# Segment-recurrent attention on one core: turns, scores and memory rows in 128x32 column tiles, the softmax's output turned by VectorE

## The chip, the cores and the metric

The kernel runs on one core of a Trainium2 chip. The metric is the device time of one execution in microseconds (us); where three runs are shown, it is their median. Engines are named as the profile names them: PE is TensorE (PEld its weight loads), DVE is VectorE, ACT is ScalarE, POOL is GpSimd, SP issues most DMAs.

A matmul on PE loads up to 128x128 stationary values (`lhsT`) and streams the columns of the moving operand (`rhs`) through them. The array can be used as smaller tiles: `tile_position=(row, column)` says which part a matmul uses. The profile writes a tile as rows * columns, so `128*32` is a matmul on all 128 rows and 32 of the 128 columns; four such tiles fit side by side.

## The reference

Two independent parts, whose outputs stand side by side. Part A is a sliding-window attention; the change does not touch it. Part B goes over 2048 tokens in 64 segments of 32, in strict order, and hands 8 memory rows from each segment to the next:

```python
for s in range(n_seg):
    xs = x[:, s * seg_len:(s + 1) * seg_len, :].copy()
    h = jnp.concatenate([mem, xs], axis=1)            # 8 + 32 tokens of width 640
    q = jnp.einsum('btd,dhe->bhte', h, Wq)            # 32 heads of 192
    k = jnp.einsum('btd,dhe->bhte', h, Wk)
    v = jnp.einsum('btd,dhe->bhte', h, Wv)
    scores = jnp.einsum('bhqe,bhke->bhqk', q, k) * scale
    scores = jnp.where(mask[None, None], scores, -1000000000.0)
    p = _softmax(scores, axis=-1)
    o = jnp.einsum('bhqk,bhke->bhqe', p, v)
    o = jnp.einsum('bhte,hed->btd', o, Wo)
    mem = o[:, :M, :].copy()
    outs.append(o[:, M:, :])
```

## The kernel before

`part_a` computes part A in about the first 150 us and loads weights for part B meanwhile. `part_b` calls `segment(s)` 64 times.

**Tokens and groups.** A segment has L = 40 tokens. Of the 32 that are projected in the segment itself (`main`), 8 are memory rows and 24 belong to x. The other 8, the last tokens of the segment, do not depend on the memory and are projected ahead for four segments at once (`ahead`, 32 tokens): once in four segments each group of Q, K and V is *renewed*, and the later segments take their 8 tokens from stored blocks (`Lb`, `Lv`); POOL copies such a block into QT or KT (L488). The 32 heads go in four groups of eight, g = 0 to 3.

**Projection** (`project32`, L443). The stationary operand is 32 tokens, the moving one 384 weight columns; four matmuls in four 128x32 column tiles make 32 tokens x 1536 columns. Five such rounds (the width 640 in chunks of 128) make 20 matmuls. The result has tokens on partitions, 32 for each of four pairs of heads. It is copied to bf16 (`to_sb`, L423).

**Turns** (`turn`, L456). Q and K are needed with head elements on partitions. Three 128x128 matmuls against an identity turn the 128x384 copy; `spread` copies the outcome into QT or KT, which hold, for each of the four pairs of heads, three chunks of 128 elements: head 0's first 128, the middle chunk with 64 elements of each head, and head 1's last 128.

**Scores** (`scores`, L515). 16 matmuls per group, eight on 128x64 tiles (the outer chunks) and eight on 64x64 tiles (the halves of the middle chunk), since each half of the middle chunk belongs to another head. The two heads of a pair lie on 64 partitions each.

**Softmax** (`softmax`, `put_p`, L522 to L540): on DVE scale and mask, maximum, subtraction; exponential on ACT; sum, reciprocal and two products on DVE, which write P. **Turn of P** (`turn_p`, L547): two 128x128 PE transposes into PSUM and a copy to PT (L423).

**Mix** (`mix`, L564): P times V, 16 matmuls on 32x128 tiles and 16 on 32x64 tiles into four PSUM tiles, copied to OT. **Output projection** (`project_out`, L578): 128x64 tiles, 320 columns, 24 matmuls per group (six pairs of chunks). **Memory rows** (`memory_rows`, L589): six matmuls turn the 8 new memory rows into HX, from which the next segment's projections start; `turn_late` for the next segment's Q follows.

**What sets the order.** PE runs in the order in which `segment` is written (`manual_schedule` for PE). On DVE, ACT, POOL and SP the framework's scheduler decides the order, and each engine then runs it strictly. Copies out of PSUM alternate between ACT and DVE by a counter (`evacuate`). PSUM buffers: 3 for projections (`ps_acc`), 4 that turns, scores, P's turn, mix and memory rows share in rotation (`ps_x`), 1 for the output (`ps_y`). QT, KT, P, PT, OT exist once. 23 weight tiles per segment (320 or 384 KB) do not fit in SBUF and are streamed from DRAM through five buffers (`get_unit`, L394), in PE's order.

## Time and profile before

| | |
|---|---|
| median of three runs | 2029.89 us (2027.99 to 2030.7) |
| the profiled execution: own time, span | 2024.66 us, 2022.8 us |
| PE busy | 1945.4 us, 96% of the span, 42512 matmuls |
| PE weight loads busy | 1243.6 us, 61% |
| DVE busy | 1128.3 us, 56% |
| ACT busy | 725.6 us, 36% |
| POOL busy | 193.6 us, 10% |
| DMA | 596.29 MB, mean 295 GB/s |
| mean granted TensorE clock | 0.994 |

How to read it: the page gives each engine's busy time, the chain of work that ended last followed back from the end, and groups of instructions by source line. A line of the timeline gives the start, the time from the first start to the last end of merged instructions, engine, source line, operation, output<-input, the tile, the size of the operand and the number of instructions; an idle time before it stands in brackets with what ended it. Matmuls are pipelined and their ends modelled, so the distance between starts says more about PE than its busy share. In a table by windows each engine has its busy time, then follow the granted clock, the busy share of the DMA engines and GB/s.

### The profile page before, as it was taken

The page shows a single profiled execution, that of the slowest core. Times are in us where ns is not written, and L with a number is a line of the kernel's source. Part 1 is how long each engine was busy: PE and PEld are TensorE (multiplying, and loading weights), DVE is VectorE, ACT ScalarE, POOL GpSimd, SP SyncE. Part 2 cuts the span into 40 slices and gives each one's busy share as a digit, 9 for nine tenths or more (in the row PEclk, how much of TensorE's full clock was granted, in tenths as well). Part 3 has the DMA queues.
Part 4 walks back from the last instruction along what each step waited for, and adds up shares of the span by engine and source line. Part 5 has one row for each costly group of instructions (what it writes and reads, how often), then busy time and mean ns, then how long its engine had stood idle before and what let it go on. Part 6 is the DMA issues. An engine that isn't in the chain of part 4 may idle for free.

```text
span 2022.8 us, 97144 instructions
## 1 busy us (share of the span) xinstructions
PE 1945.4 (96%) x42512; PEld 1243.6 (61%) x42512; DVE 1128.3 (56%) x3622; ACT 725.6 (36%) x2126; POOL 193.6 (10%) x674
## 2 busy tenths in 40 slices
PE   7989999999999999999999999999999999999998
PEld 4656666666666666666666666666666665666665
DVE  5875555555555455555555555555555554555554
ACT  3543333333333333333333333333333333333333
POOL 2000000110001101001001001101001001110110
PEclk9999999999999999999999999999999999999999
DMA  9927999999899999999999989999899988989997
GB/s 343 311 76 269 311 300 305 301 302 307 290 305 304 299 288 312 302 304 303 303 299 297 308 292 311 305 303 299 296 298 303 298 304 284 303 293 300 305 302 257
DMA packets 270123, 596.29 MB, mean 295 GB/s; under 512 B 61065, under 2 KB 72841, under 8 KB 269385
## 3 DMA queue, kind: packets, MB, share of 16 engines
q1 hardware_dynamic: 264770, 585.97, 87.9%
q8 instruction: 333, 5.46, 1.1%
q0 software_dynamic: 4928, 4.11, 0.6%
q14 instruction: 92, 0.75, 0.1%
HBM read 576.85 MB, written 18.87 MB: 295 GB/s over the span
## 4 chain that ended last, share of the span: by engine, by line
PE 71%; DMA 19%; DVE 6%; ACT 1%; issue 1%; SPq 1%; POOL 0%; DVEq 0%; POOLq 0%; ACTq 0%
PE acc L443 33%; PE Y L578 18%; DMA t<-wcopy_k 8%; DMA t<-wcopy_o 6%; PE pt L456 6%; PE Sps L515 4%; PE OTps L564 4%; PE pq L95 2%; PE pt L547 2%; DVE sb L423 2%; DMA out_dram<-row 2%; DMA t<-wcopy_v 1%; PE po L161 1%; DMA wcopy_o<-in_B_Wo_dram 1%; PE py L172 1%
## 5 line engine op out<-in xcount | busy, mean ns | idle before, releaser
L443 PEld LDWEIGHTS <-HX 128*32 128x32 bf16 x19380 | 462.7, 96 | 274.3 <-issue 46.5
L578 PEld LDWEIGHTS <-OT 128*64 128x64 bf16 x6144 | 316.8, 109 | 131.0 <-ACT OT L423 20.0
L578 PE MATMUL Y<-wres_o,OT 128*64 128x320 bf16 x3584 | 344.3, 302 | 2.2
L443 PE MATMUL acc<-wres_q,HX 128*32 128x384 bf16 x6460 | 332.6, 328 | 0.5 <-ACT sb L423 0.2
L443 PE MATMUL acc<-t,HX 128*32 128x384 bf16 x4200 | 309.1, 328 | 12.9 <-DMA t<-wcopy_k 10.1
L578 PE MATMUL Y<-t,OT 128*64 128x320 bf16 x2560 | 277.7, 303 | 10.0 <-DMA t<-wcopy_o 9.2
L423 DVE CAST sb<-acc 128x384 bf16<-128x384 f32 x322 | 178.8, 556 | 186.6 <-PE acc L443 171.3
L443 PE MATMUL acc<-wres_v,HX 128*32 128x384 bf16 x4844 | 276.5, 328 | 0.1
L528 ACT ACTIVATE t<-t 128x160 f32<-128x160 f32 x256 | 86.1, 336 | 439.4 <-DVE t L527 439.4
L443 PE MATMUL acc<-wres_k,HX 128*32 128x384 bf16 x3876 | 224.8, 327 | 0.3 <-issue 0.3
L522 DVE SCALAR_TENSOR_TENSOR t<-Sps,mask 128x160 f32<-128x160 f32 x256 | 82.8, 323 | 214.6 <-PE Sps L515 186.6
L423 ACT CAST sb<-acc 128x384 bf16<-128x384 f32 x324 | 153.6, 474 | 125.1 <-PE acc L443 123.5
L456 PE MATMUL pt<-ident,sb 128*128 128x128 bf16 x1938 | 179.4, 221 | 6.9 <-DVE sb L423 1.7
L423 DVE CAST OT<-OTps 128x120 bf16<-128x120 f32 x512 | 125.5, 271 | 97.4 <-PE OTps L564 96.8
L488 POOL COPY QT<-Lb 128x96 bf16<-128x96 bf16 x252 | 67.4, 267 | 1112.0 <-PE Sps L515 955.2
L456 PEld LDWEIGHTS <-sb 128*128 128x128 bf16 x1938 | 110.2, 97 | 82.3 <-issue 32.3
L515 PEld LDWEIGHTS <-QT 128*64 128x64 bf16 (+1 forms) x4096 | 118.9, 109 | 55.1 <-issue 40.5
L423 ACT CAST OT<-OTps 128x120 bf16<-128x120 f32 x512 | 106.0, 258 | 110.7 <-PE OTps L564 110.4
L515 PE MATMUL Sps<-KT,QT 128*64 128x40 bf16 (+1 forms) x4096 | 137.0, 188 | 2.2 <-DVE KT L423 1.0
L530 DVE TENSOR_REDUCE sm<-t 128x4 f32<-128x160 f32 x256 | 81.8, 320 | 78.7 <-ACT t L528 78.7
L564 PEld LDWEIGHTS <-Vst 32*128 32x128 bf16 (+1 forms) x4096 | 62.2, 97 | 82.3 <-issue 60.5
L564 PE MATMUL OTps<-PT,Vst 32*128 32x40 bf16 (+1 forms) x4096 | 109.7, 192 | 0.0
(75 smaller groups left out, 1916.0 us busy)
## 6 DMA issues: line engine op xcount, KB each, us to landing
t<-wcopy_o SPq DMA_DIRECT2D x640, 320.0 KB, 4.3
t<-wcopy_k SPq DMA_DIRECT2D x512, 384.0 KB, 4.8
t<-wcopy_v SPq DMA_DIRECT2D x320, 384.0 KB, 4.8
wres_q<-in_B_Wq_dram SPq DMA_DIRECT2D x20, 384.0 KB, 7.7
wres_v<-in_B_Wv_dram SPq DMA_DIRECT2D x15, 384.0 KB, 7.8
wres_k<-in_B_Wk_dram SPq DMA_DIRECT2D x12, 384.0 KB, 7.7
wres_o<-in_B_Wo_dram SPq DMA_DIRECT2D x14, 320.0 KB, 6.7
wcopy_o<-in_B_Wo_dram SPq DMA_DIRECT2D x10, 320.0 KB, 8.1
```

What stands on the lines that cost most here:

```text
L95: nc.tensor.matmul(pq[32 * d:32 * d + 32], lhsT=wcol[:, k, t, 4 * c + d, :], rhs=xTs[s][:, k, :], start=(k == 0), stop=(k == 4), tile_posi ...
L423: (nc.scalar.copy if copies["n"] % 2 else nc.vector.tensor_copy)(dst, src)
L443: nc.tensor.matmul(ps[n][32 * j:32 * j + 32, :], lhsT=X[:, dc, :], rhs=w[:, 384 * j:384 * j + 384], start=(dc == 0), stop=(dc == 4), tile_ ...
L456: nc.tensor.matmul(pt[:, c], lhsT=sb[:, 128 * c:128 * c + 128], rhs=ident, start=True, stop=True)
L488: nc.gpsimd.tensor_copy(tokens(T)[:, :, 32:L], b[:])
L515: nc.tensor.matmul(Sps[64 * g2:64 * g2 + 64, a, :], lhsT=QT[lo:hi, L * cc:L * cc + 64], rhs=KTt[lo:hi, cc, :], start=(g2 not in seen), sto ...
L522: nc.vector.scalar_tensor_tensor(out=t1[:], in0=Sps[:], scalar=scale, in1=mask[:].unsqueeze(1).to_broadcast([128, 4, L]), op0=ALU.mult, op ...
L528: nc.scalar.activation(t1[:], t1[:], ACTF.Exp)
L530: nc.vector.tensor_reduce(out=sm[:], in_=t1[:], axis=AX.X, op=ALU.add)
L547: nc.tensor.transpose(pt[:, late, :], P[:, late].rearrange("p a n -> p (a n)"), ident)
L564: nc.tensor.matmul(dst, lhsT=V[32 * a:32 * a + 32, e0:e1], rhs=PT[32 * a:32 * a + 32, late, half, :], start=(wide and late == 0 and half = ...
L578: nc.tensor.matmul(Y[64 * gv:64 * gv + 64, :], lhsT=OT[:, L * c:L * c + 64], rhs=w[:, n:n + 320], start=(i == 0 and r == 0), stop=(i == 23 ...
```

## The change

- `turn` makes each 128x128 turn in four matmuls on 128x32 column tiles (`turn32`), twelve per call in place of three. For K, the middle chunk's halves are directed to different places, so that the output's lower 64 partitions hold the chunks in one order and the upper 64 in another.
- KT is now [128, 4, 4, L]: the middle chunk of a pair of heads is kept twice, with zeros in the half that belongs to the other head (KT is cleared once at the start). `spread` therefore fills KT with two copies of 64 partitions each, where there was one of 128; POOL's copies of stored K blocks double in the same way.
- `scores` uses 128x32 column tiles alone: 32 matmuls per group, on full 128 rows. The 40 tokens of a head lie as two blocks of 32 rows (tokens 0 to 31; 32 to 39 and 24 unused rows) on the 32 partitions of a pair of heads. The mask is laid out to match.
- P has the same layout, so that a 32x32 block transpose on DVE (`nc.vector.transpose`, 128x256) makes PT in SBUF. `turn_p`, its PE transposes and its copies are gone; `put_p` returns PT.
- `memory_rows` uses 20 matmuls on 128x32 tiles in place of six on 128x128 and 128x64.
- In `segment`, `put_p` of groups 1, 2 and 3 stands behind the mix of the group before; the calls of `turn_p` are gone.

```diff
-    mask = cpool.tile([128, L], FP32)
+    mask = cpool.tile([128, 2, L], FP32)
...
-    KT = cpool.tile([128, 12 * L], BF16, name="KT")
+    KT = cpool.tile([128, 4, 4, L], BF16, name="KT")
-    P = cpool.tile([128, 2, 4, 32], BF16, name="P")
+    P = cpool.tile([128, 2, 2, 2, 32], BF16, name="P")
...
+    nc.gpsimd.memset(KT[:], 0.0)
...
-    def turn(sb):
+    def turn32(dsts, src):
+        for j in range(4):
+            nc.tensor.matmul(dsts[j][32 * j:32 * j + 32, :], lhsT=src[:, 32 * j:32 * j + 32], rhs=ident, start=True,
+                             stop=True, tile_position=(0, 32 * j))
+
+    LOW, HIGH = (1, 0, 2), (0, 2, 1)
+
+    def turn(sb, m):
         pt = ps_x.tile([128, 3, 4, 32], FP32, tag="x")
+        at = [pt[:, c].rearrange("p j n -> p (j n)") for c in range(3)]
         for c in range(3):
-            nc.tensor.matmul(pt[:, c], lhsT=sb[:, 128 * c:128 * c + 128], rhs=ident, start=True, stop=True)
+            lo, hi = (at[LOW[c]], at[HIGH[c]]) if m == "k" else (at[c], at[c])
+            turn32((lo, lo, hi, hi), sb[:, 128 * c:128 * c + 128])
         return pt
...
+    def heads(m, n0, n1):
+        if m == "q":
+            return [tokens(QT)[:, :, n0:n1].rearrange("p (j c) n -> p j c n", c=3)]
+        return [KT[0:64, :, 0:3, n0:n1], KT[64:128, :, 1:4, n0:n1]]
+
+    def spread(dsts, src):
+        for d, dst in enumerate(dsts):
+            part = src if len(dsts) == 1 else src[64 * d:64 * d + 64]
+            evacuate(dst.rearrange("p j c n -> p c j n"), part)
...
-        Sps = ps_x.tile([128, 4, L], FP32, tag="x")
...
+        Sps = ps_x.tile([128, 2, 2, L], FP32, tag="x")
+        plan = [(kind, g2, part) for kind in range(2) for g2 in range(2) for part in range(2)]
+        for n, (kind, g2, part) in enumerate(plan):
+            for a in range(4):
+                c = 3 * a + g2 + part
+                at = L * c + 32 * kind
+                nc.tensor.matmul(Sps[32 * a:32 * a + 32, g2, kind, :], lhsT=QT[:, at:at + 32],
+                                 rhs=KT[:, a, ((1, 0), (3, 2))[g2][part], :], start=(n == 0), stop=(n == len(plan) - 1),
+                                 tile_position=(0, 32 * a))
...
-    def turn_p():
-        pt = ps_x.tile([128, 2, 128], BF16, tag="x")
-        for late in range(2):
-            nc.tensor.transpose(pt[:, late, :], P[:, late].rearrange("p a n -> p (a n)"), ident)
-        PT = one.tile([128, 2, 2, L], BF16, tag="PT")
-        evacuate(PT[:], pt[:].rearrange("p l (h n) -> p l h n", h=2)[:, :, :, 0:L])
+        PT = one.tile([128, 2, 2, 64], BF16, tag="PT")
+        nc.vector.transpose(PT[:].rearrange("p l g n -> p (l g n)"), P[:].rearrange("p l g k n -> p (l g k n)"))
         return PT
...
-        for dc in range(5):
-            for gv in range(2):
...
+        for n in range(20):
+            gv, j = n // 10, n % 4
+            nc.tensor.matmul(pt[32 * j:32 * j + 32, n // 4, :], lhsT=Ysb[:, 32 * n - 320 * gv:32 * n - 320 * gv + 32],
+                             rhs=ident[:, 64 * gv:64 * gv + M], start=True, stop=True, tile_position=(0, 32 * j))
...
-        put_p(s, 0, *softmax(scores(0)))
+        PT[0] = put_p(s, 0, *softmax(scores()))
...
-        PT[0] = turn_p()
-        put_p(s, 1, *soft)
         tk[2] = project_qk(s, "k", 2)
         mix(0, PT[0], V[0])
+        PT[1] = put_p(s, 1, *soft)
         V[1] = values(s, 1)
         tk[2]()
-        PT[1] = turn_p()
```

Groups 2 and 3 change in the same way.

## Prediction

> **What bounds the kernel now.** I read the page first (busy shares, slices, chain), then the order of time on PE, DVE's order of time, last the DMA windows.
>
> ```profile
> span 2022.8 us, 97144 instructions
> PE 1945.4 (96%) x42512; PEld 1243.6 (61%) x42512; DVE 1128.3 (56%) x3622; ACT 725.6 (36%) x2126; POOL 193.6 (10%) x674
> PE 71%; DMA 19%; DVE 6%; ACT 1%; issue 1%; SPq 1%; POOL 0%; DVEq 0%; POOLq 0%; ACTq 0%
> ```
>
> PE carries the chain. Part B has 64 segments; the copy of the memory rows marks them:
>
> ```profile
> L592 DVE CAST HX<-pt x63: 199/200/202, 217.2 to 1990.5; 128x40 bf16<-128x40 f32 x63
> ```
>
> 62 steps in 1773.3 us are 28.60 us a segment. A busy PE is not a full PE, so I looked at starts (first column) in one segment:
>
> ```profile
> 1015.26 0.34 PE L456 MATMUL pt<-ident,sb 128*128 128x128 bf16 x3
> 1015.53 1.00 PE L443 MATMUL acc<-wres_q,HX 128*32 128x384 bf16 x20
> 1016.36 0.34 PE L443 MATMUL acc<-t,HX 128*32 128x384 bf16 x4
> ...
> 1020.08 0.50 PE L443 MATMUL acc<-t,HX 128*32 128x384 bf16 x8
> 1020.51 0.55 PE L515 MATMUL Sps<-KT,QT 128*64 128x40 bf16 x16
> 1020.99 0.68 PE L456 MATMUL pt<-ident,sb 128*128 128x128 bf16 x9
> ```
>
> Twenty projection matmuls start every 0.041 (0.83/20): four column tiles side by side. Turns add 0.057 each (0.34 for three, 0.68 for nine), so three should end 0.17 after their start; the next projection starts 0.27 after. Eight projections need 0.33, yet the scores follow after 0.43. Wherever the tile shape changes, about 0.10 passes with nothing running. A change inside one group:
>
> ```profile
> 1002.82 0.22 PE L564 MATMUL OTps<-PT,Vst 32*128 32x40 bf16 x8
> 1002.88 0.21 PE L564 MATMUL OTps<-PT,Lv 32*128 32x40 bf16 x8
> 1003.02 0.23 PE L564 MATMUL OTps<-PT,Vst 32*64 32x40 bf16 x8
> 1003.07 0.20 PE L564 MATMUL OTps<-PT,Lv 32*64 32x40 bf16 x8
> 1003.21 0.83 PE L443 MATMUL acc<-wres_v,HX 128*32 128x384 bf16 x16
> ```
>
> The step within one shape is 0.06, across the shapes 0.14. 32 matmuls with their 32 weight loads pass in 0.39, two such changes included. The turn of P inside an output projection:
>
> ```profile
> 1009.88 0.44 PE L578 MATMUL Y<-wres_o,OT 128*64 128x320 bf16 x4
> 1010.25 0.28 PE L547 MATMUL pt<-ident,P 128*128 128x128 bf16 x2
> 1010.47 0.33 PE L578 MATMUL Y<-wres_o,OT 128*64 128x320 bf16 x2
> ```
>
> 0.59 from output group to output group instead of 0.27.
>
> **The change, part by part (us per segment).**
>
> *Changes of shape.* In the program's order I count 39 per segment before. After it, turns, scores and memory rows have the projections' shape, and 20 are left (around the four mixes, three output projections and the two scores that border one). Of the 19 that go, three lie around the memory rows, where PE waits for the cast of Y anyway (30.2 in total, 0.47 a segment): I credit 0.1 there. The other 16 at 0.10: **-1.6**, and -0.1 at the end.
>
> *P on VectorE.* Eight matmuls of 0.057 leave PE: **-0.45**. Four copies of P leave (DVE 0.234 or ACT 0.292 each), four DVE transposes of 256 columns come. None is in the trace; DVE rows give 0.187 for 32 elements, 0.289 for 128, 0.320 for 160, 0.556 for 384, so 0.29 to 0.56, and by the line through them 0.42, which I take. The transpose also waits until the mix before has read PT; what stands behind it on DVE then is that mix's output or V, which come no earlier. PE's waits for P (two rows, 6.1 and 13.9, 0.3 a segment) mostly go: **-0.2**, the rest moves to the mix.
>
> *Scores.* 16 matmuls in two shapes become 32 in one. Without the two changes they take 0.25 now. Bounds for 32 in eight rounds of four: 0.009 each (the mix without its changes: 0.28) down to 0.005, the streaming of 40 columns at the projections' rate, and up to 0.023 (the row above, 0.36/16): 0.15 to 0.74. I take 0.19, near the low end, because four column tiles side by side is what the projections do: 4 x -0.06 = **-0.2**.
>
> *Turns and memory rows.* Three matmuls become twelve, in three rounds of 128 columns: 384 columns take a round 0.163, 128 a third, 0.055. Ten turns a segment: **0**. Memory rows, 20 for 6, go into the wait for Y: 0. Both with the same upper bound as the scores.
>
> Together **-2.4**. Now what is late next.
>
> *The copy of the second K projection.* In the row above it ends at 1020.58, a DVE cast of it runs 1020.70 to 1021.26, and its turn can start at 1021.31, 0.90 after PE streamed the last column (1020.41). PE fills that now with scores (0.48 with changes), a turn (0.17) and its first change, 0.75. After: 0.19 + 0.17. So 0.4 of the gain comes back as a wait: **+0.4**. The scores before it meet a K that is now copied in two halves (0.55 on DVE, 0.48 on ACT, side by side, but one behind the cast of Q): up to 0.3, inside the same wait.
>
> *The copy of the third Q projection.* In the built program DVE runs it behind the reciprocal of the first softmax:
>
> ```profile
> 1021.18 0.32 DVE L522 SCALAR_TENSOR_TENSOR t<-Sps,mask 128x160 f32<-128x160 f32 x1
> 1022.01 0.55 DVE L423 CAST KT<-pt 128x384 bf16<-128x384 f32 x1
> 1023.54 0.18 DVE L531 RECIPROCAL sm<-sm 128x4 f32<-128x4 f32 x1
> ```
>
> 2.36 from the first row to the reciprocal, with three casts between, 0.18, cast 0.48 in the stream, 0.05: 3.05 after the softmax begins. PE now gets there in wait, turn, two projections (1.63) and scores: 2.5 to 2.7. **+0.3**, in three of four segments.
>
> *Slots.* A mix holds four of four ps_x buffers; the next turn needs the first back, and its copy is behind the second softmax on DVE: **+0.2**. Half K copies ahead of the third and fourth scores: **+0.1**. POOL's copies into K double (189 more of 0.27), early in a stretch of over 2 us between scores: 0. If that cover were gone, 0.3.
>
> *DMA.* PE waits 21 in all for tiles. The columns end with DMA share and GB/s:
>
> ```profile
> 180.00:205.00 25.00, 23.41 (x552) 14.90 (x544) 12.78 (x44) 9.10 (x28) 0.00 (x0) 1.00 1.02 364
> 245.00:1990.00 1745.00, 1700.11 (x38553) 1088.97 (x38554) 957.00 (x3325) 608.63 (x1861) 171.62 (x610) 1.00 0.92 301
> 1712.00:1722.00 10.00, 9.56 (x214) 5.72 (x214) 6.41 (x25) 3.70 (x12) 0.95 (x4) 0.83 0.73 237
> ```
>
> A segment's 8.6 MB need 28.6 at 301 GB/s; at 364 they would need 23.7. At 27.2 the rate is 316. Five buffers, refilled as PE frees them, will be late more often: **+0.2** (0 to 1.0). The last row: after two waits of together 1.6 PE ran a while at half clock; more waits may cause more of that, some 1.7 each, kept for the range.
>
> Sum: -2.4 - 0.2 + 0.4 + 0.3 + 0.2 + 0.1 + 0.2 = **-1.4**; x 64 = -90. Once: POOL has six more mask instructions of 0.5 and clears K before the first segment: +2. So -88. The profiled execution took 2024.7 (span 2022.8), 5.2 under the median 2029.9, from which I count: **1942**.
>
> **Rivals.**
>
> *A floor per matmul (slower).* PE gets 52792 matmuls for 42512. If short ones in column tiles do not overlap but cost f each, scores, ten turns and memory rows cost 32f x 4 + 12f x 10 + 20f = 268f against 2.58 now assumed. At f = 0.023, the scores row with its inner change, +3.6 against -2.4: +1.2, 2107. It decides from f = 0.019. For it: the scores row. Against: the mix at 0.009, the projections' four side by side. Chance 0.11.
> The Trainium skill states this rule (TensorEngine Tiling (Array Packing), Performance Considerations): about 60 cycles of overhead per matmul, so do not tile a dimension that is already small; TensorE: Matmul & The Clock Gate, Back-to-back issue gap, gives 25 ns. By that figure an estimate is +1.7 a segment, 2139. The mix row speaks against it, for tiles that run side by side.
>
> *DVE and ACT take it all.* DVE gets 256 transposes and 34 more copies, and in the first 14 us of a segment it has nearly no gaps left. If the casts come 1.3 later than counted: 2025, a little either way. For it: the cast of the third Q waits for a whole softmax. Against: DVE is 56% busy. 0.10.
>
> *DMA ends it.* If the rate stays near 310 as steady stretches show, 8.6 MB need 27.8: -0.8, 1979. Against: 364 above. 0.17.
>
> *Nothing comes back.* Copies land in time: -2.4 and a little: 1880. Against: the 0.90 above. 0.10.
>
> **How the numbers follow.** My forecast has 0.52. 1885 to 2025 leaves out the floor, half of the case "nothing comes back" and the upper side of the copies: 0.2. The forecast's own range: give-backs of 0.4 to 1.8 make 1900 to 1990. 0.2%, 4 us, is about what tells from no change. Faster: 0.52 + 0.17 + 0.10 less noise: 0.77; same 0.04; slower: floor 0.11, copies, clock: 0.19.
>
> **What would show it.** Twelve turn matmuls in 0.17 and 32 scores in about 0.2 (floor: 0.3 and 0.7); turn to projection without a gap; waits of PE's loads for casts (sb, KT) up from 17 to 40 or more; DMA near 316 GB/s; a transpose of 0.4. I am wrong if the waits for casts exceed 1.5 a segment, or if the scores take over 0.5.

## The result, and the profile after

The changed kernel takes 2125.08 us in the median of 4 runs (2121.87 to 2136.71), the kernel before 2028.94 (2025.42 to 2030.70): a ratio of 1.0486, 95% interval 1.0444 to 1.0529. It is slower by 96 us, 1.5 us a segment, where 1942 us was forecast. A rival had nearly this time (a floor per matmul, 2107), but not for its reason, as will be seen.

The page of the kernel after: the span, the engines, two DMA queues, and the chain that ended last by engine.

```profile
span 2123.5 us, 117872 instructions
PE 1856.0 (87%) x52792; PEld 1226.2 (58%) x52792; DVE 1288.7 (61%) x3912; ACT 759.9 (36%) x2159; POOL 245.1 (12%) x872
...
q1 hardware_dynamic: 264770, 585.97, 83.9%
q8 instruction: 412, 6.75, 1.3%
...
PE 55%; DVE 17%; issue 12%; DMA 9%; ACT 6%; SPq 0%; POOL 0%; ACTq 0%; DVEq 0%; POOLq 0%
```

PE is busy for 89 us less than before (1945.4) although it gets 10280 matmuls more, yet the span is 101 us longer. So PE's busy time did become shorter, and PE stands still for some 190 us more. The chain says where to look: PE fell from 71% to 55%, DMA from 19% to 9%, while DVE rose from 6% to 17% and "issue", time in which PE waited for nothing that the profile can name, from 1% to 12%.

The waits of PE's weight loads and of its matmuls in the kernel after (what for, us in total, how many, the longest):

```profile
PEld L446 <- issue: 123.2, 230, 3.0
PEld L579 <- issue: 87.8, 264, 2.5
PEld L534 <- issue: 78.0, 125, 3.3
PEld L534 <- ACT KT L426: 49.5, 90, 1.0
...
PEld L534 <- DVE KT L426: 19.9, 44, 0.6
...
PE acc L446 <- issue: 52.9, 64, 2.7
PE Sps L534 <- ACT KT L426: 50.1, 99, 2.4
PE Sps L534 <- issue: 25.9, 31, 3.2
...
PE Sps L534 <- DVE KT L426: 6.0, 20, 0.3
```

There are two new stories. The scores (line 534) wait for the two half copies of K. (Loads and matmuls wait at the same time in part; with that counted once, the K rows of both lists, 125.5 us, are 101 us, 1.6 us a segment.) And there are waits for "issue" of up to 3.3 us in every kind of work. Before, the weight loads of the projections had 46.5 us of such waits, the longest 1.1. One of the long ones, from the order of time after (start, length, engine, line; in brackets the idle time before and what ended it):

```profile
245.09 0.12 PEld L579 LDWEIGHTS <-Vst 32*128 32x128 bf16 x8 [0.25 <-issue]
245.13 0.10 PEld L579 LDWEIGHTS <-Lv 32*128 32x128 bf16 x3
247.69 0.11 PEld L579 LDWEIGHTS <-Lv 32*128 32x128 bf16 x5 [2.46 <-issue]
247.69 0.21 PE L579 MATMUL OTps<-PT,Lv 32*128 32x40 bf16 x5 [2.36 <-issue]
```

PE stops in the middle of a mix, after three of eight equal weight loads whose operands are all there, and goes on 2.5 us later. The explanation offered here, and tested below, is that it has run out of instructions. The queue q8 tells how they come: 412 packets and 6.75 MB are 16384 B each, and 2 x 52792 PE instructions over 412 are 256 a packet. Before, it was 333 packets. In the trace's packet records a packet of q8 starts at 245.30, right behind the stop, takes 0.93 us, and PE goes on 1.5 us after its end. Of the 86 gaps of over 1 us between the starts of PE's instructions in part B (240 to 1980 us) 66 end 1.15 to 1.65 us behind the end of a q8 packet, where chance would give one in ten; before there are 4 gaps of that size. All gaps over 0.3 us that end so make 172 us after and 12 before.

The Trainium skill (Runtime: NRT & Kernel Launch, Instruction fetch mechanics) describes this: an engine's instructions come in 16 KiB blocks of 256, the sequencer fetches the next block while it executes the current one, and the cost at a block's end is "mostly hidden". The trace agrees on the block and not on the last point: hidden before, not after.

K's copies, in the groups by line and in the order of time after:

```profile
L426 ACT CAST KT<-pt 64x384 bf16<-64x384 f32 (+1 forms) x323 | 136.6, 423 | 127.2 <-DVE KT L426 73.0
...
1040.06 0.54 DVE L426 CAST KT<-pt 64x384 bf16<-64x384 f32 x1
1040.69 0.47 ACT L426 CAST KT<-pt 64x384 bf16<-64x384 f32 x1
```

ACT's half starts when DVE's has ended: 73.0 us of ACT's idle time ends with the other half's copy. They run one behind the other, 1.1 us in all, not side by side. The trace's records also point at the reason: in all 252 pairs of full half copies in part B the second one carries a wait on a semaphore that the first one's engine raises, and none of the pairs overlap. So the order is most likely laid down in the built program, without the kernel's text asking for it (the records lack the semaphores' values); whether the two engines could read one PSUM tile at once was not tried.

**Where a segment's time went.** This table is worked out from PE's records: the time from the start of one matmul to the start of the next, summed by the function of the two over 58 segments, us a segment. "To" is the step from another function's last matmul to the first of this one, and holds the changes of shape and most waits, but also the time of that last matmul: twelve narrow matmuls in place of three move some of a turn's time from the step behind it into the row "turns", so these rows are to be read together. Two kernels described below, with the streamed weights cut to an eighth, stand beside the two.

```
                       before   before_light   after   after_light
projections             11.16      10.77       12.30      10.82
output projections       6.09       5.87        6.27       5.98
mix                      1.12       1.12        1.57       1.39
scores / to scores    1.41/0.83   1.41/0.82  1.34/1.99   0.84/2.40
turns / to turns      1.47/1.28   1.47/1.26  1.99/0.94   1.60/1.09
P's turn / to it      0.30/0.68   0.29/0.59      -           -
memory rows              0.30       0.30        0.12       0.12
to projections           1.41       1.39        0.94       0.85
other steps              2.55       2.54        2.59       2.61
sum                     28.60      27.83       30.05      27.70
```

### The profile page after: what moved, and what is told of

Its sections match the earlier page's. It is cut to its first block, busy times and chain, and to the rows that moved or that the text cites. A ratio compares the mean times of both kernels' runs of the same rounds, so it can differ in the third digit from the quotient of the medians.

```text
span 2123.5 us, 117872 instructions
## 1 busy us (share of the span) xinstructions
PE 1856.0 (87%) x52792; PEld 1226.2 (58%) x52792; DVE 1288.7 (61%) x3912; ACT 759.9 (36%) x2159; POOL 245.1 (12%) x872
## 3 DMA queue, kind: packets, MB, share of 16 engines
q8 instruction: 412, 6.75, 1.3%
## 4 chain that ended last, share of the span: by engine, by line
PE 55%; DVE 17%; issue 12%; DMA 9%; ACT 6%; SPq 0%; POOL 0%; ACTq 0%; DVEq 0%; POOLq 0%
PE acc L446 27%; PE Y L593 11%; DVE KT L426 4%; DMA t<-wcopy_k 4%; PE Sps L534 4%; PE pt L459 4%; PE OTps L579 4%; PE pq L95 3%; DMA t<-wcopy_o 2%; ACT KT L426 2%; DMA out_dram<-row 2%; DVE t L547 2%; ACT sb L426 1%; PE po L161 1%; DVE t L541 1%
## 5 line engine op out<-in xcount | busy, mean ns | idle before, releaser
L446 PEld LDWEIGHTS <-HX 128*32 128x32 bf16 x19380 | 509.1, 97 | 296.3 <-issue 123.2
L446 PE MATMUL acc<-t,HX 128*32 128x384 bf16 x4200 | 324.7, 330 | 20.4 <-issue 10.4
L426 DVE CAST sb<-acc 128x384 bf16<-128x384 f32 x355 | 195.0, 549 | 123.9 <-PE acc L446 115.4
L459 PE MATMUL pt<-ident,sb 128*32 128x128 bf16 x7752 | 192.6, 221 | 40.4 <-issue 22.8
L426 ACT CAST sb<-acc 128x384 bf16<-128x384 f32 x291 | 138.6, 476 | 168.0 <-PE acc L446 155.4
L459 PEld LDWEIGHTS <-sb 128*32 128x32 bf16 x7752 | 138.3, 96 | 78.6 <-issue 28.5
L426 ACT CAST KT<-pt 64x384 bf16<-64x384 f32 (+1 forms) x323 | 136.6, 423 | 127.2 <-DVE KT L426 73.0
L534 PE MATMUL Sps<-KT,QT 128*32 128x40 bf16 x8192 | 107.6, 181 | 84.4 <-ACT KT L426 50.1
L534 PEld LDWEIGHTS <-QT 128*32 128x32 bf16 x8192 | 86.5, 94 | 153.4 <-issue 78.0
L426 DVE CAST KT<-pt 64x384 bf16<-64x384 f32 (+1 forms) x323 | 157.1, 486 | 19.4 <-ACT KT L426 8.3
```

Of the source, the lines that this page charges most:

```text
L426: (nc.scalar.copy if copies["n"] % 2 else nc.vector.tensor_copy)(dst, src)
L446: nc.tensor.matmul(ps[n][32 * j:32 * j + 32, :], lhsT=X[:, dc, :], rhs=w[:, 384 * j:384 * j + 384], start=(dc == 0), stop=(dc == 4), tile_ ...
L459: nc.tensor.matmul(dsts[j][32 * j:32 * j + 32, :], lhsT=src[:, 32 * j:32 * j + 32], rhs=ident, start=True, stop=True, tile_position=(0, 32 ...
L534: nc.tensor.matmul(Sps[32 * a:32 * a + 32, g2, kind, :], lhsT=QT[:, at:at + 32], rhs=KT[:, a, ((1, 0), (3, 2))[g2][part], :], start=(n == ...
```

## The experiments

Theory 1: TensorE gets its instructions too late; a block of 256 takes a certain time to come, and the change makes the blocks pass faster than that. Theory 2: K's two copies in a row are what costs. Rivals: a floor per matmul, and DMA that ends the segments. Runs of the kernel before on the same chip stand in brackets; where two variants ran on different chips, the difference of their times is good to some 10 us only (the kernel before itself took 2028 to 2039 us by chip).

### How fast instructions come

**before_tail**: narrow matmuls behind the last segment of the kernel before; each narrow(n, cols) issues n matmuls of cols columns in 128x32 tiles, with nothing to wait for.

```diff
...
+        for n in range(48):
+            t = wstream.tile([128, SLOT], BF16, tag="ws", name="w_tail")
+            nc.sync.dma_start(t[:], copied[("k", n % 4, 0)])
+        for cols in (8, 128, 8, 128):
+            narrow(1024, cols)
```

> The kernel before with four stretches of 1024 narrow matmuls put behind the last segment, all on 128x32 tiles, nothing to wait for in them: 8 columns, 128 columns, 8 columns, 128 columns; 48 whole weight tiles (18.9 MB, some 52 us at 364 GB/s) are loaded beside the first of them. Theory 1, instruction supply: a TensorE instruction stream can't be fed faster than one block of 256 instructions in about 3.4 us (the shortest interval between its fetches in either trace is 3.4 to 3.8 us). A stretch is 2048 instructions, 8 blocks: 27 us each, whatever the width, with the 0.7 to 3 us gaps at every 256th instruction. Rival, a floor per matmul or no limit: the stretches go at the rate of the memory rows (20 in 0.124 us, so 6.3 us for 1024 of 8 columns) and of the turns (0.055 us for four, so 14 us for 128 columns), without such gaps. If the fetch is slowed by the weight transfers, the first stretches are longer than the last ones; if its latency is fixed, they are equal.

The stretches took 39.6, 34.1, 30.0 and 30.0 us. Order of time on PE, four blocks beside full weight streams, and, below the dots, three with idle DMA engines (the last one cut off by the end of the window):

```profile
2028.98 1.19 PE L658 MATMUL pt_tail<-ident,OT 128*32 128x8 bf16 x128 [4.49 <-issue]
2033.82 1.19 PE L658 MATMUL pt_tail<-ident,OT 128*32 128x8 bf16 x128 [3.65 <-issue]
2040.03 1.19 PE L658 MATMUL pt_tail<-ident,OT 128*32 128x8 bf16 x128 [5.02 <-issue]
2044.88 1.19 PE L658 MATMUL pt_tail<-ident,OT 128*32 128x8 bf16 x128 [3.65 <-issue]
...
2098.86 1.20 PE L658 MATMUL pt_tail<-ident,OT 128*32 128x8 bf16 x128 [2.29 <-issue]
2102.88 1.19 PE L658 MATMUL pt_tail<-ident,OT 128*32 128x8 bf16 x128 [2.83 <-issue]
2106.63 0.55 PE L658 MATMUL pt_tail<-ident,OT 128*32 128x8 bf16 x51 [2.56 <-issue]
```

128 matmuls with their 128 weight loads, one block, are executed in 1.2 us, and then PE waits for the next. The windows of these stretches (the last columns are the granted clock, the DMA share and GB/s):

```profile
2022.00:2061.00 39.00, 9.22 (x986) 8.45 (x982) 0.00 (x0) 0.43 (x1) 0.98 (x2) 0.54 0.98 350
2096.00:2125.00 29.00, 8.91 (x962) 8.21 (x951) 0.00 (x0) 0.00 (x0) 0.00 (x0) 0.51 0.02 5
2126.00:2155.00 29.00, 18.30 (x978) 16.71 (x968) 0.00 (x0) 0.00 (x0) 0.00 (x0) 0.86 0.02 5
```

Width does not matter: 8 and 128 columns take the same 30 us. From resume to resume a block takes 3.8 us with idle DMA engines (mean of 7) and 5.4 beside full streams (mean of 6). The packet records split it: from PE's resume to the start of the next fetch 1.1 to 1.7 us idle, 2.2 to 3.8 loaded; the packet itself 0.9 to 1.4 in both; from its end to the resume 1.2 to 1.6 in both. So it is the start of the fetch that the weight streams delay. In these stretches no fetch starts before PE has taken up the block that came last, which fits one block ahead and no more.

### Without the streams

**before_light** and **after_light**: the same edit in both kernels, a streamed tile loads 16 of its 128 rows and keeps an earlier load in the others; **after_half_rows**: 64 rows in place of 16.

```diff
...
-        nc.sync.dma_start(t[:, 0:unit_cols(u)], copied[u])
+        n = loads["n"]
+        loads["n"] += 1
+        if n < nbuf:
+            slots.append(wstream.tile([128, SLOT], BF16, name=f"ws{n}"))
+            nc.sync.dma_start(slots[n][:], copied[("k", 0, 0)])
+        t = slots[n % nbuf]
+        nc.sync.dma_start(t[0:16, 0:unit_cols(u)], copied[u][0:16])
```

> After, with the streamed weight tiles loading 16 of their 128 partitions (the rest of a tile keeps an earlier load, so the results of part B are not the reference's); every PE instruction stays, nearly all waits for weights go. Theory 1 with a fixed latency of the fetch: the 182 gaps over 0.7 us (210 us) stay within a fifth, and the time stays over 2060. If the fetch is late only since it shares the DMA engines with the weights: the gaps fall to under a third, and the time comes near 1960. A DMA that ends the segments (chain: 9%) without any supply limit would give some 2125 - 0.09 x 2123 = 1930 to 1950 as well, but with the gaps unchanged in place.

> The kernel before with the same light streams, as the control of the one above. Its chain had DMA at 19% and issue at 1%: with the weights' waits gone some 1920 to 1980 in every theory. What tells apart is the distance of after_light from it: over 100 us if PE's instructions or the K copies are what costs (both theories), under 40 if the DMA engines make the difference between the two kernels.

> After, with the streamed weight tiles loading 64 of their 128 partitions. If the fetch waits in proportion to the DMA engines' load: half way between after_light (1971) and after (2125), 2030 to 2065. If only streams at their full rate hold it up, when the five slots are refilled one behind the other: the DMA engines are idle half of the time, and it is near after_light, 1971 to 2010.

after_light took 1971.19 us, before_light 1977.75 (before 2039.39); after_half_rows 2007.92 (before 2037.98). Busy time and chain of before_light (first two lines) and after_light:

```profile
PE 1926.7 (98%) x42512; PEld 1237.5 (63%) x42512; DVE 1127.0 (57%) x3622; ACT 725.7 (37%) x2126; POOL 192.9 (10%) x674
PE 90%; DVE 7%; ACT 1%; issue 1%; DMA 1%; SPq 0%; POOL 0%; POOLq 0%; DVEq 0%; ACTq 0%
```

```profile
PE 1804.1 (92%) x52792; PEld 1210.4 (61%) x52792; DVE 1277.2 (65%) x3912; ACT 758.9 (39%) x2159; POOL 246.0 (12%) x872
PE 48%; DVE 31%; ACT 9%; issue 8%; DMA 2%; SPq 1%; ACTq 0%; DVEq 0%; POOL 0%; POOLq 0%
```

The streams cost the kernel before 62 us and the kernel after about 154 (its 2125.08 was measured on another chip). Without them the change is worth 6.6 us. No theory had given that: the two kernels differ by under 40 us, which the expectation put down to the DMA engines, and the DMA engines are indeed the lever; but PE's waits for tiles are not the way (11 us in the kernel after, 20 before, in 240 to 1900 us). The gaps between matmuls of over 0.7 us tell it: 23 before (20 us), none in before_light, 182 after (210 us), 93 in after_light (86 us), and 90 of those 93 stand ahead of scores or turns: waits for copies, not at the ends of blocks. At half the bytes the loss is 37 us of the 154: it is not in proportion to the bytes, and three quarters of it come with the second half of them.

This pair also shows the natural pace of the blocks, the interval between two fetches when PE does not run dry: median 5.55 us in before_light, 4.31 in after_light. Set against 3.8 to 5.4 us for the coming of a block, the kernel before stays mostly above, the kernel after mostly below.

### The second copy of K

**k_one_copy** leaves out the half copy of partitions 64 to 127; **k_one_copy_light** does so with light streams.

```diff
-            evacuate(dst.rearrange("p j c n -> p c j n"), part)
+            if d:
+                copies["n"] += 1
+            else:
+                evacuate(dst.rearrange("p j c n -> p c j n"), part)
```

> After, with the second of K's two half copies (partitions 64 to 127) left out; the scores then lack the upper half of K. Theory 2, the two copies of one turned K tile run one behind the other and PE waits for the second: PE waited 119.5 us for K's copies, 1.9 us a segment, and most of the second one's 0.5 us comes off 4 score groups a segment: 60 to 120 us, so 2005 to 2065. Theory 1 alone, instruction supply: the PE instructions are the same, the gaps move but stay, and the time is above 2100.

> After with both the light weight streams (16 of 128 partitions) and without the second half copy of K (the upper half of K is left out of the scores, and most of the streamed weights are not renewed). With full streams, leaving out the copy gained nothing (2147 against 2125), since the supply took its place; with light streams the supply is out of the way (the 93 gaps over 0.7 us that are left are waits for K's copies ahead of the scores). If the second copy is the next limit below the supply: 1971 less most of the 86 us of these gaps, 1880 to 1910. If PE or the softmax is: 1950 or more.

k_one_copy took 2147.09 us (before 2039.39, ratio 1.0539, 1.0466 to 1.0612): no gain over the kernel after (1.0486, 1.0444 to 1.0529). k_one_copy_light took 1915.94 (before 2035.18), 55 us under after_light. Waits in k_one_copy, of PE's weight loads and matmuls:

```profile
PEld L446 <- issue: 139.9, 219, 2.4
PEld L582 <- issue: 106.2, 277, 2.7
PEld L537 <- issue: 67.9, 166, 2.5
PEld L459 <- issue: 47.0, 47, 3.2
PEld L537 <- DVE KT L426: 18.3, 33, 2.1
...
PE acc L446 <- issue: 64.8, 77, 2.0
PE Sps L537 <- DVE KT L426: 8.2, 15, 1.7
```

The waits for K are down to 27 us from 126, and the waits for issue have grown ahead of projections, mixes and turns (the loads' 123.2, 87.8 and 28.5 us became 139.9, 106.2 and 47.0); those of the scores' loads fell from 78.0 to 67.9. Of 98 gaps over 1 us 87 end 1.15 to 1.65 us behind a fetch. The copies are a real wait, and the next one below the supply; with full streams taking it away only lets PE run dry sooner. Theory 2 alone does not set the time of the kernel after.

### Fewer instructions, at the price of changes of shape

**turns_64**: the turns in 128x64 tiles.

```diff
-        for j in range(4):
-            nc.tensor.matmul(dsts[j][32 * j:32 * j + 32, :], lhsT=src[:, 32 * j:32 * j + 32], rhs=ident, start=True,
-                             stop=True, tile_position=(0, 32 * j))
+        for j in range(2):
+            nc.tensor.matmul(dsts[2 * j][64 * j:64 * j + 64, :], lhsT=src[:, 64 * j:64 * j + 64], rhs=ident, start=True,
+                             stop=True, tile_position=(0, 64 * j))
```

> After, with its turns in 128x64 column tiles: 6 matmuls a turn in place of 12, the same layout, copies and scores. TensorE instructions fall from 2 x 52792 to 2 x 48916, some 412 blocks of 256 to 382, 6.45 to 5.98 a segment; but each turn now stands between two changes of shape again. Theory 1, sharpened by the runs before this one: a block of 256 TensorE instructions takes 3.7 us with idle DMA engines and up to 5.3 with full ones (the tail's stretches), 4.68 in after, and after is bound by 6.45 x 4.68 = 30.2 us a segment. So 5.98 x 4.7 to 5.0 = 28.0 to 29.9 us: faster than after by 20 to 130 us, 1995 to 2105, though the shapes change more often. Rival, the shapes and K copies alone: some 12 changes more a segment at 0.08 us less 60 matmuls at 0.014 is slower than after by some 10 to 60 us, 2135 to 2185.

**k_padded_64**: K's zeros come from the turn (four chunks, 8 matmuls), and one copy of 128 partitions goes to KT. To make room, the mask is kept in bf16 and there are fewer stored blocks for K, each of 16 chunks.

```diff
...
+    CH = {"q": 3, "k": 4}
+    PARTS = {"q": ((0, 1), (2, 3), (4, 5)), "k": ((0, 1), (2, None), (None, 3), (4, 5))}
...
+                src = none[:, 0:1].to_broadcast([128, 64]) if part is None else sb[:, 64 * part:64 * part + 64]
...
-        return [KT[0:64, :, 0:3, n0:n1], KT[64:128, :, 1:4, n0:n1]]
+        return [KT[:, :, :, n0:n1]]
```

> After, with K's zeros put in by the turn and not by the two half copies: K's turn has four chunks (first, middle low with zeros, middle high with zeros, last), in 128x64 tiles, 8 matmuls, and goes to KT by one copy of 128 partitions; Q's turn has 6. Everything is computed. About 1550 TensorE instructions a segment, 6.05 blocks. Theory 1: 6.05 x 4.7 to 5.0 = 28.4 to 30.3 us, so 2020 to 2125, no better than turns_64 although K is copied once. Theory 2, K's two copies in a row are what costs: 1.9 us a segment less than after, and 0.5 more for changes of shape, 2020 to 2050, and some 60 to 100 under turns_64.

turns_64: 2085.67 us (before 2035.18; ratio 1.0249, 1.0220 to 1.0278), faster than the kernel after by 2.4 points although the shape changes more often. k_padded_64: 2086.27 (1.0265, 1.0230 to 1.0299). PE's waits for K in turns_64, loads first:

```profile
PEld L534 <- ACT KT L426: 39.6, 78, 0.9
PEld L534 <- DVE KT L426: 29.8, 57, 0.6
...
PE Sps L534 <- ACT KT L426: 41.9, 96, 2.8
```

In k_padded_64 they are 4.6 us in all:

```profile
PEld L537 <- DVE KT L428: 3.0, 12, 0.3
PE Sps L537 <- DVE KT L428: 1.6, 1, 1.6
```

Two kernels with 382 and 388 blocks, one with over 110 us of waits for K and the other with under 5, take the same time, where theory 2 had the second 60 to 100 us faster. That speaks for theory 1, though the two differ in more than the copy: k_padded_64 has six blocks more and two more matmuls in each turn of K.

### One part of the change alone

**before_turns_32**: the kernel before with 12 matmuls in 128x32 tiles for a turn's three; **before_turns_32_light**: the same with light streams.

```diff
-            nc.tensor.matmul(pt[:, c], lhsT=sb[:, 128 * c:128 * c + 128], rhs=ident, start=True, stop=True)
+            for j in range(4):
+                at = 128 * c + 32 * j
+                nc.tensor.matmul(pt[32 * j:32 * j + 32, c], lhsT=sb[:, at:at + 32], rhs=ident, start=True, stop=True,
+                                 tile_position=(0, 32 * j))
```

> The kernel before with one part of the change alone: its turns in 128x32 column tiles, 12 matmuls in place of 3; scores, K and P as before, K is not kept twice. Instructions 2 x 42512 to 2 x 48326, 377 blocks, 5.9 a segment. By the prediction's step for the shapes alone, some 15 changes fewer a segment at 0.08 us, less 0.1: 1940 to 1965. Theory 1: the blocks want 5.9 x 4.7 to 5.0 = 27.7 to 29.5 us, so most of that gain is taken by the supply: 1975 to 2060, with issue waits several times those of before (20 us).

> The kernel before with its turns in 128x32 tiles and the light weight streams (16 of 128 partitions, so part B's weights are mostly not renewed); to be held against before_light (1977.8) as before_turns_32 (2080.3) against before (2035.2). By the prediction's step for the shapes, some 15 changes fewer a segment at 0.08 us: 1900 to 1925. By what the traces of the light runs show by line (between lines 6.60 us a segment in before_light; a turn's 12 matmuls longer than its 3 by 0.14 us a segment): the narrow turns win 0.1 to 0.3 us a segment, 1958 to 1972. In both it is faster than before_light, and the sign turns with full streams; if it is slower here too, the narrow turns themselves cost, and not the supply.

before_turns_32: 2080.31 us (ratio 1.0215, 1.0169 to 1.0261), slower than before by 45 (its interval lies on both sides of 2%); 378 blocks, 65 gaps over 0.7 us (70 us) in place of 23 (20 us). With light streams 1984.60, 6.9 us slower than before_light (another chip; by the traces 0.07 us a segment, 4 us), where both expectations had it faster. So nearly 40 of the 45 us go with the streams, and by the gaps with the supply; but the gain for the shapes is not there either. The step table of the light runs shows why: the steps to projections fall by 0.26 us and those to turns by 0.18, but the steps to P's turn, still 128x128 behind a narrow turn now, grow by 0.28, those to scores by 0.07, and the row of the turns grows by 0.18 (part of which has only moved there from the steps to projections). A change of shape is not removed if the neighbour on the other side keeps its own.

### Does the place matter?

**extra_sparse** and **extra_dense** put 48 idle matmuls a segment into the kernel before, in Q 0, K 0, Q 1 or in Q 2, V 0, K 2 (in fact 56 and 52 on average: the condition also holds for Q of the group that is projected ahead at the end of a segment, in two and in one of four segments); **before_edge_turns** has narrow turns only about the boundary of two segments, **before_edge_32** the narrow memory rows as well. In the first diff EXTRA names the three projections, in the second a turn whose last argument is true has the twelve narrow matmuls.

```diff
+            if (m, g) in EXTRA and dc:
+                for j in range(4):
+                    nc.tensor.matmul(ps[-1][32 * j:32 * j + 32, 384:392], lhsT=Xs[-1][:, dc, :],
+                                     rhs=w[:, 384 * j:384 * j + 8], start=False, stop=False, tile_position=(0, 32 * j))
```

```diff
-        pt = turn(sb)
+        pt = turn(sb, start > s or g == 0)
...
-            pt = turn(sbs[-1])
+            pt = turn(sbs[-1], g == 0)
```

> The kernel before with 48 idle matmuls a segment put in (128x32 tiles, 8 columns, four ahead of each projection round but a group's first, into unused columns of the same PSUM bank; nothing reads them), in the first three projections of a segment (Q 0, K 0, Q 1), where 256 instructions took 6.5 us in before_light. 24 blocks more. Their own price at the memory rows' rate (6.2 ns) to twice that is 0.3 to 0.6 us a segment, 2050 to 2070, by theory 1 by place as by the rival.

> The same 48 idle matmuls in three other projections of the segment (Q 2, V 0, K 2), where 256 instructions took 4.7 to 5.5 us in before_light, less than or as much as a fetch beside full streams. Theory 1 by place: their own price and 0.4 to 1 us a segment of waits for instructions, 25 to 65 us slower than extra_sparse. Rival, the number alone: as extra_sparse within 10 us.

> The same without the memory rows: only the three or four turns about the boundary are in 128x32 tiles; some 29 matmuls more a segment, 5.43 blocks. Theory 1 by place: two to three changes fewer, 0.2 us a segment, 2010 to 2025, between before and before_edge_32. Rival, the number alone: 14 blocks more, 2040 to 2055.

> The kernel before, with 128x32 column tiles only about the boundary of two segments: memory rows (20 matmuls for 7), the turn of the next Q and the turns of the first Q and K (12 for 3); all the rest as before. Some 42 matmuls more a segment, 5.2 to 5.5 blocks. There 256 instructions take 6 to 6.6 us in before_light, longer than the 5.3 us of a fetch beside full streams. Theory 1 by place: the supply doesn't bind there, and the gain of the shapes stays, some 5 changes fewer at 0.08 us = 0.4 us a segment: 1998 to 2020, faster than before. Rival, the number of instructions alone (1.2 us for each block more than the 333 of before, as the four kernels with full streams lie): 20 blocks more, 2050 to 2060.

extra_sparse 2058.36 us (ratio 1.0157, 1.0134 to 1.0180), extra_dense 2061.16 (1.0170, 1.0147 to 1.0193): the same within the intervals, where the theory by place wanted 25 to 65 us between them. before_edge_turns 2031.22 (1.0026, 1.0010 to 1.0042), before_edge_32 2039.63 (1.0067, 1.0048 to 1.0086): neither the gain that the theory by place gave nor the loss of the rival. So neither holds in the form stated. The gaps over 0.7 us between matmuls, by tenths of a segment, counted from one copy of the memory rows (the cast to HX) to the next, over 62 segments:

```
tenth of the segment     0   1   2   3   4   5   6   7   8   9
before                   -   1   6   -   2   2   2   3   2   5
before_edge_32           5  16   7   2   1   2   4   3   1   2
extra_sparse             2  14   1   3   1   4   2   1   2   3
extra_dense              4   1   5   8   2   5   3   3   2   3
after                    2  61  30  17  13  15  15  19   5   2
after_light (waits)      -  46  18  11   -   -  15   1   -   1
```

The added matmuls lie in tenths 9 to 1 in before_edge_32, mostly in 0 in extra_sparse, and in 2 and 3 in extra_dense. The gaps come up in the same tenth or the one behind it, which is what a supply one block ahead would do. But they are few, 16 to 31 us a kernel more than before, and do not differ between the two places. What the added matmuls cost by themselves can be read from the starts: a projection round of four takes 0.163 us, and 0.188 with four idle matmuls ahead of it. 14 and 13 such rounds a segment are 0.35 and 0.33 us, 22 and 21 us a kernel. That leaves 8 and 12 us of the 30 and 33 for everything else, about as much as the gaps grew (16 and 19 us), so in these two kernels some 26 blocks more cost little. Within this family, no version with full streams was faster than the kernel before.

All kernels with full streams, by their blocks (packets of q8) and the gaps over 0.7 us (in turns_64 and after some are waits for K):

```
                    blocks   gaps    us    time over before, us
before                333     23     20      -
before_edge_turns     347     26     27      3
before_edge_32        354     42     51     12
extra_dense           359     36     39     33
extra_sparse          361     34     37     30
before_turns_32       378     65     70     45
turns_64              382    104    107     50
k_padded_64           388     93    112     51
after                 412    182    210     96
k_one_copy            413    178    226    108
```

### Smaller packets

**after_halves**, **before_halves**, **k_padded_64_halves** load each streamed tile by two DMAs of half the columns, **after_quarters** by four.

```diff
-        nc.sync.dma_start(t[:, 0:unit_cols(u)], copied[u])
+        part = unit_cols(u) // 2
+        for i in range(2):
+            nc.sync.dma_start(t[:, part * i:part * i + part], copied[u][:, part * i:part * i + part])
```

> After, with each streamed weight tile loaded by two DMAs of half the columns in place of one: the same bytes, in packets of 1536 and 1280 B (0.07 us) in place of 3072 and 2560 B (0.121 and 0.102 us). The tail showed a fetch of 256 instructions starting 1.2 us after PE took up the block before with idle DMA engines, and 2.2 to 3.8 us after it beside full weight streams. Theory 1a, it waits behind a number of weight packets on its DMA engine: the wait halves, a block takes some 4.4 us in place of 5.3 under full load, and after comes down by 40 to 90 us, 2035 to 2085. Theory 1b, it waits behind bytes (or for its share of the bandwidth): 2115 to 2135, fetch intervals as before. Rival: smaller packets cost the weights their rate (under 281 GB/s), and it is slower than 2135.

> The same edit in the kernel before, whose issue waits are 20 us and whose chain has DMA at 19%. Theory 1a: at most those 20 us come off, 2010 to 2035; theory 1b: no change, 2025 to 2040; if the rate of the weights falls by its smaller packets, the DMA share of the chain grows and it is slower than 2040.

> After with each streamed tile in four DMAs of a quarter of the columns, packets of 768 and 640 B. Theory 1a: the wait of the fetch shrinks again, some 15 to 40 us under after_halves. Theory 1b: as after_halves. If packets of this size cost rate (they carry less per packet of about 0.04 us), slower than after.

> The variant with K's zeros put in by an eight-matmul turn (one copy of K, 2086.3) with weights in halves. It has no second K copy and fewer instructions, so if theory 1a holds it can use what the fetch gives back: 2000 to 2050, and it may pass before; under theory 1b 2080 to 2095.

2208.93, 2135.52, 3491.99 and 2184.41 us, in this order (before 2032.93): all worse, halves by 4 to 5 points in every kernel. The chain of before_halves, and SP's order of time in after_halves:

```profile
PE 56%; DMA 34%; SPq 4%; DVE 3%; issue 2%; ACT 1%; POOL 0%; POOLq 0%; DVEq 0%; ACTq 0%
```

```profile
1000.18 5.96 SPq L396 DMA_DIRECT2D t<-wcopy_o  x10
```

DMA took a larger part of the chain (34%, 19% in the kernel before), and SP needs about 0.6 us for each of ten DMAs in a row: with 46 a segment in place of 23 it would be occupied for most of a segment. The smaller packets cost rate as well, as the expectation's rival had it: a packet of 1536 B took 0.065 us against 0.121 for 3072 B, 1280 B 0.055 against 0.102, so the same bytes occupy the DMA engines 7 to 8% longer. Which of the two costs the halves their time was not parted; with quarters SP has 26% of the chain, with halves 4%. Either way the edit made the weights slower before it could probe the fetch. It says nothing for or against the fetch waiting behind packets. That before_halves lost as much suggests that the weight streams of the kernel before have little room either.

## Why the prediction was wrong

**The gain was about right.** The prediction took 2.4 us a segment off PE, and 0.2 off its waits for P. Between before_light and after_light, where the streams are out of the way, five rows of the table get shorter by 2.34 together: P's turn and the steps to it 0.88, scores 0.57, steps to projections 0.54, memory rows 0.18, steps to turns 0.17. The turns' own row gets longer by 0.13, so 2.2 is left of the 2.6. Its parts came out otherwise than listed. The scores go at 0.21 a group (0.84 / 4; 0.19 forecast, in the kernel after 0.34 with stalls), a DVE transpose takes 0.44 (0.42 forecast), four turn matmuls side by side are as cheap as the projections' four. The count of 16 changes at 0.10 was not confirmed one by one: narrow turns alone won nothing.

**First failed step: "K that is now copied in two halves (0.55 on DVE, 0.48 on ACT, side by side ...): up to 0.3, inside the same wait", and +0.1 for the third and fourth scores.** The copies run one behind the other, the second with a wait on the first one's engine, and all four score groups wait for the later half. The steps to the scores are 1.16 us a segment longer than before, 1.58 with light streams, in place of 0.4 at most. The sign had been in the trace of before: there, too, ACT's copies of late blocks from one PSUM tile were released by DVE's copies from the same tile, 60.8 us of ACT's idle time. The prediction itself set the mark, "wrong if the waits for casts exceed 1.5 a segment": for the casts of K alone they are 125.5 us in the two lists, 1.96 a segment, or 101 us, 1.6 a segment, with overlaps counted once. The waits forecast ahead of turns (+0.4 for the second K projection's copy, +0.3 for the third Q's) came out smaller: PE's and its loads' waits of turns for casts to sb rose from 19.5 to 40.7 us, 0.3 a segment, and the steps to turns became shorter.

**Second failed step, the larger one: there was none for the instructions.** The terms for turns and memory rows (0) and for the scores (-0.2) priced some 160 matmuls more a segment by the time that they occupy PE, and nothing by what it takes to bring them: some 320 instructions, 5.2 blocks a segment becoming 6.45. By the sums of the table the streams cost 0.77 us a segment before and 2.35 after, 1.58 us a segment or 100 us more (the figure is by chance the same as that of the K copies). The gaps that end with a fetch (172 us against 12 before, and 33 in after_light, about what chance gives there) put most of that on the supply: one in ten of all gaps would end so by chance. It is spread over work that the change does not touch, as a shortage is: projections +1.48, scores +0.50, turns +0.39, output +0.29, mix +0.18 between after_light and after. It takes the place of part of the waits for K (steps to the scores -0.41).

The sum of the steps as measured: -2.34, then +1.58 for K's copies, +0.27 in the mix (0.2 forecast for the ps_x slots), +0.36 for longer turns, output and other steps, -0.13 without the streams; +1.58 for the supply; 1.45 a segment, 93 us of the 96.

**The rivals.** *A floor per matmul* gave 2107 for a wrong reason: 32 scores take 0.21 us and a turn's rounds are no longer than forecast where instructions are at hand. It was near, since a price per instruction exists; but it is paid where a block runs out, not at each matmul, and in this kernel only beside the streams. *DVE and ACT take it all*: half right, the chain shows DVE at 17%, through K. *DMA ends it*: PE's waits for tiles fell; the window of part B after shows the streams slower, since PE frees the slots later:

```profile
245.00:1990.00 1745.00, 1532.40 (x45903) 1018.11 (x45900) 1051.85 (x3417) 609.00 (x1795) 206.50 (x751) 0.99 0.87 286
```

286 GB/s at a share of 0.87 (301 at 0.92 before; 316 was forecast). *Nothing comes back* at 1880 would have needed light streams and one copy of K: 1916 in k_one_copy_light. The *half clock* kept for the range is at most small: 0.99 granted in place of 1.00 over 1745 us, an estimate of 17 us at the most.

**What could have been seen.** The page of before has a queue of 333 instruction packets, and the trace of before has them 5.6 us apart in the median, 3.8 in the fastest hundredth, with a few PE waits of about 1 us for "issue". A fetch interval that is already near its shortest, set against a quarter more instructions, asks for a term of its own.

**What stays open.** Why the fetch starts later beside full streams: whether it waits behind a number of packets, behind bytes or for a share of a DMA engine. The halves were to tell and did not. The Trainium skill (DMA: Bandwidth & Descriptors, Queues, rings and completion order) states that a DMA engine serves its queues in turn and drains some 9 to 17 descriptors of one before it goes on to the next; with 0.121 us for a 3072 B entry of the weights in the trace that would be an estimate of 1.1 to 2.1 us of waiting, near the 1.7 us by which the loaded fetches of the tail start later (2.9 on average against 1.3). No run here isolates it. Nor was it tried whether the two copies from one PSUM tile could run at once without the semaphore between them. And no rule was found that gives a variant's loss from its number of blocks and their place: theory 1 by place and the count alone both missed for the edge kernels.

## What to carry to other kernels

Count TensorE's instructions as a resource with a rate of its own. Here a block of 256 came every 3.8 us in the mean with idle DMA engines, and every 5.4 us beside weight streams of 350 GB/s; in this kernel, cutting matmuls into four for the sake of their shape did not pay once the blocks passed faster than that. To test for such a limit, run both kernels once with the big transfers cut down: a change that is good only there is being paid for in the fetch. And two copies from one PSUM tile are to be costed one behind the other until a trace shows them side by side; whether a semaphore of the program orders them can be looked up in the trace.

## What was not expected of the hardware

- Instruction fetches of TensorE show as 16384 B packets on a DMA queue, one block ahead; in the stretches behind the last segment PE resumes 1.2 to 1.6 us after a packet's end, and the fetch starts 1.1 to 1.7 us after a resume with idle DMA engines, 2.2 to 3.8 beside full streams.
- With half of the streamed bytes only 37 of the 154 us of loss remain.
- SP took 5.96 us for ten weight DMAs in a row, and a packet of half the size took 0.065 us, not half of 0.121: with tiles loaded in halves the whole kernel took 4 to 5% longer, and in quarters 3492 us.
